# A gated recurrence in halves of 64 tokens: 64x64 scores, and one contraction of 128 rows for the output

## The chip, the cores and the metric

One core of one Trainium2 chip. The time is device microseconds of one execution; what is compared is the median of several executions. A profile is one execution of the same program with the hardware profiler on, and its span is 1 to 2 us shorter than the time on the clock (before: span 646.0, time 647.7). A run is called fast when it lies within 1.5% of the fastest of its kernel. In the profile PE is the matrix engine (TensorE), PEld its weight loads, the granted clock the share of its full clock that PE was given, DVE the vector engine, ACT the scalar engine, POOL GpSimd, and SP the engine whose queue issues most loads.

## The reference, cut to what matters

```python
batch, n_heads, seq, head_dim = (4, 8, 768, 48)
f = 1.0 / (1.0 + np.exp(-f_logit))
for t in range(S):
    state = f[:, :, t, :, None] * state + k_t (outer) v_t      # 48x48 per head
    y[:, :, t] = q_t @ state
x = y, as 3072 tokens x 384
h = x @ w_in                                   # 384 -> 2048
g = h * erf(softplus(h))
out = g @ w_out                                # 2048 -> 384
```

All in 32-bit floats. The recurrence is a small part of the arithmetic, but it feeds everything behind it.

## The kernel before

The 768 tokens of a sequence are cut into 6 chunks of 128; there are 24 chunks, and 3 of them make a block of 384 tokens, the unit of the feed-forward part. Per chunk there are four stages: decays (`stage_d`: a sum over tokens by a matmul with a triangle, then two exponentials), transposes of q' and k' (`stage_t`), scores and state (`stage_s`) and the output y (`stage_y`). With C the sum of the log decays, q' = q exp(C) and k' = k exp(-C), so that masked scores q'k' give the part of y from inside the chunk and q' times the state the rest.

```python
def stage_s(g):
    for a in range(HP):                      # 4 pairs of heads
        for r in range(2):                   # head of the pair
            nc.tensor.matmul(sc[:, r, a, :], lhsT=kT[rows(r), a, :], rhs=qT[rows(r), a, :], ...)   # 48 rows, 128x128
    nc.vector.tensor_tensor(out=A, in0=sc, in1=tri, op=ALU.mult)       # the mask, 128x1024
    if c == NCH - 1:
        return                                # no state after the last chunk
    for a in range(HP):
        for r in range(2):
            nc.tensor.matmul(dS[rows(r), a, :], lhsT=kd[:, h, 0:D], rhs=vt[:, a, r, 0:D], ...)      # 128 rows
    for r in range(2):
        nc.vector.tensor_tensor(out=Sn, in0=dS, in1=old, op=ALU.add)
        nc.gpsimd.tensor_tensor(out=new, in0=Sn, in1=total, op=ALU.mult)  # total: decay over the chunk

def y_matmuls(...):      # out x token, 32 columns of x at a time on four column tiles
    terms.append((pair[:, o : o + M], A[:, r, a, :]))             # v with scores, 128 columns
    if Mbd is not None:
        terms.append((flat[:, M * part : M * (part + 1)], qT[:, a, :]))   # state with q'
```

`total` comes for block 0 from small matmuls, later from rows of exp(C) that eight small DMAs per two chunks carry across partitions (`Tall`).

The feed-forward part is `hidden` (matmuls `hps`, from x) and `project` (matmuls `ops`). The recurrence of block n+1 is laid between the matmuls of block n's hidden and block n-2's project, at fixed slots; the activations and the logits of block n+2 (`prepare`: exp, then ln) are laid there too.

```python
todo = deque(stages(blk))                # the stages of the next block
at = [int(3 + (n - 13) / len(todo) * i) for i in range(len(todo))]   # their slots, n = 96
...
if it + 2 < n_blocks and s == (16 if it < 2 else 30):
    prepare(it + 2, 0, CPB)
```

At the start the weights are loaded and rounded in pieces by DVE, ACT helping; that work, with the early chunks, keeps DVE busy for 116 of the first 139.5 us.

Of the kernel before, what the change touches and what calls it, by code (L numbers as in the profile page):

```python
# [69 lines left out]
def kernel(  # L71
# [19 lines left out]
    M = 32  # L91
    NCH = S // P
# [16 lines left out]
    tri = fixed("tri", [P, P])  # L109
    w_in_sb = fixed("w_in_sb", [P, n_k, d_ff])  # L110
# [58 lines left out]
    epool = main.enter_context(tc.tile_pool(name="epool", bufs=3))  # L169
# [6 lines left out]
    vts = [fixed(f"vt{i}", [P, HP, 2, DP], pool=fix) for i in range(NV)]  # L176
# [5 lines left out]
    Mbds = [fixed(f"Mbd{i}", [P, HP, 2, D], pool=fix) for i in range(2)]  # L182
    Tall = fixed("Tall", [P, n_chunks, HP], pool=fix)
# [16 lines left out]
    def load(g, what="qkv", queue=None):  # L200
        b, c = divmod(g, NCH)
        queue = queue or nc.sync
        for src, t, n in ((q, qns[g % NQ], "q"), (k, kns[g % NQ], "k")):
            if n in what:
                queue.dma_start(out=t[:].rearrange("t (h d) -> t h d", d=D), in_=heads(src, b, c))
        if "v" in what:
            queue.dma_start(
                out=vts[g % NV][:].rearrange("t a r d -> t (a r) d")[:, :, 0:D], in_=heads(v, b, c)
            )

# [80 lines left out]
    xTs, As, qTs, kTs = {}, {}, {}, {}  # L291
# [35 lines left out]
    def stage_d(g):  # L327
        blk, j = divmod(g, CPB)
        if blk == 0:
            both = ps_moe.tile([P, 2, 512], FP32, name="ps_d0", tag="moe")  # L330
            ps, totals[g] = both[:, 0, 0:d_model], both[:, 1, 0:HP]
# [11 lines left out]
        if blk > 0:  # L343
            for a in range(HP):
                nc.sync.dma_start(
                    out=Tall[:, g, a : a + 1],
                    in_=dp[P - 1 : P, 2 * a : 2 * a + 2, :].rearrange("o r d -> o (r d)"),
                )
# [8 lines left out]
    def stage_t(g):  # L357
        pss = []
# [8 lines left out]
        qTs[g] = work.tile([P, HP, P], FP32, name="qT", tag="qT")  # L367
        kTs[g] = work1.tile([P, HP, P], FP32, name="kT", tag="kT")
        nc.scalar.copy(out=qTs[g][:], in_=pss[0][:])  # L369
# [4 lines left out]

    def stage_s(g):
        b, c = divmod(g, NCH)
        qT, kT = qTs[g], kTs.pop(g)
        sc = ps_sc.tile([P, 2, HP, P], FP32, name="sc", tag="sc")
        for a in range(HP):
            for r in range(2):  # L380
                nc.tensor.matmul(  # L381
                    sc[:, r, a, :], lhsT=kT[rows(r), a, :], rhs=qT[rows(r), a, :],
                    start=True, stop=True,
                )
        if g in totals:

            pairs = dps[g % 2][:].rearrange("t (a r) d -> t a (r d)", r=2)
            for a in range(HP):
                nc.tensor.matmul(  # L389
                    totals[g][:, a : a + 1], lhsT=pairs[:, a, :], rhs=ident[:, P - 1 : P],  # L390
                    start=True, stop=True,
                )
            nc.vector.tensor_copy(out=Tall[:, g, :], in_=totals.pop(g))
        A = work1.tile([P, 2, HP, P], FP32, name="A", tag="A")
        nc.vector.tensor_tensor(  # L395
            out=A[:].rearrange("s r a t -> s (r a) t"),
            in0=sc[:].rearrange("s r a t -> s (r a) t"),
            in1=tri[:].unsqueeze(1).broadcast_to((P, H, P)),
            op=ALU.mult,
        )  # L400
        As[g] = A
        if c == NCH - 1:
            return
        dS = ps_at.tile([P, HP, D], FP32, name="dS", tag="at")
        vt, kd = vts[g % NV], kds[g % 2]
        for a in range(HP):
            for r in range(2):
                h = 2 * a + r
                nc.tensor.matmul(  # L409
                    dS[rows(r), a, :], lhsT=kd[:, h, 0:D], rhs=vt[:, a, r, 0:D],  # L410
                    start=True, stop=True,
                )
        new, old = Mbds[g % 2], Mbds[(g + 1) % 2]
        Sn = work1.tile([P, HP, D], FP32, name="Sn", tag="Sn")
        for r in range(2):
            total = Tall[rows(r), g, :].unsqueeze(2).broadcast_to((D, HP, D))
            if c == 0:
                nc.vector.tensor_tensor(
                    out=new[rows(r), :, r, :], in0=dS[rows(r)], in1=total, op=ALU.mult
                )  # L420
                continue
            nc.vector.tensor_tensor(  # L422
                out=Sn[rows(r)], in0=dS[rows(r)], in1=old[rows(r), :, r, :], op=ALU.add
            )
            nc.gpsimd.tensor_tensor(  # L425
                out=new[rows(r), :, r, :], in0=Sn[rows(r)], in1=total, op=ALU.mult
            )

    def stage_y(g):
        c = g % NCH  # L430
# [6 lines left out]
        y_matmuls(y, As.pop(g), vts[g % NV], qTs.pop(g), Mbds[(g + 1) % 2] if c else None)  # L437
        nc.scalar.copy(out=xTs[blk][:, :, j * P : (j + 1) * P], in_=y[:])  # L438

# [3 lines left out]
    def activate(gr):  # L443
# [17 lines left out]
        for _ in range(n):  # L461
# [4 lines left out]
        yield  # L466
# [3 lines left out]
    LEAD = len(SERF_KAB) + 2  # L470
# [89 lines left out]
    def check_decays():  # L560
# [3 lines left out]
            out=low[:], in_=Tall[:].rearrange("p g a -> p (g a)"), axis=AX.X, op=ALU.min  # L564
# [11 lines left out]
    with tc.manual_schedule():  # L576

        use_exp_ln()
# [5 lines left out]
        load_f(2)  # L584
        load_piece(0)
        load(1, "v")
        load(2)
        load_piece(1)
# [7 lines left out]
        )  # L596
        make_identity(nc, ident)
# [4 lines left out]
        for t in vts:  # L602
            nc.vector.memset(t[:, :, :, D:DP], 0.0)
        for t in Mbds:
            nc.vector.memset(t[:], 0.0)
# [56 lines left out]
        stage_y(0)  # L662
        load(3, "v")
# [6 lines left out]
        prepare(1, 0, CPB)  # L670
        load(4, "v")
# [4 lines left out]
        stage_y(2)  # L676
        load(5, "v")
# [271 lines left out]
```

## Time and profile before

| | before |
|---|---|
| time, median (lowest to highest) | 647.45 us (647.44 to 647.85) |
| span of the profile, granted clock | 646.0 us, 0.999 |
| first hidden matmul of block 0 starts at | 32.4 us |
| DVE's last rounding of weights ends at | 139.5 us |

The lines that the prediction rests on stand in it. Three more serve to compare. First the stretch 143 to 197 us, from the table of stretches (length, then busy us of PE, PEld, DVE, ACT, POOL, then granted clock, DMA share, GB/s):

```profile
143.00:197.00 54.00, 53.68 (x321) 33.65 (x322) 41.81 (x35) 46.34 (x40) 7.29 (x6) 1.00 0.17 37
```

PE is idle for 0.3 us in it. Then PE's order of work where hidden of block 0 begins (start, length, engine, line, what, idle time before it):

```profile
32.41 2.85 PE L497 MATMUL hps<-xT,w_in_sb 128*128 128x384 f32 x8 [0.61 <-ACT xT L438]
```

Eight records in 2.85 us. And the loads at the start of the SP queue (start, time the queue spends on issuing, what, how many):

```profile
8.09 0.49 SPq L207 DMA_DIRECT2D vt<-in_v_dram  x1
```

### The profile page before, as it was taken

The page shows a single profiled execution, that of the slowest core. Times are in us where ns is not written, and L with a number is a line of the kernel's source. Part 1 is how long each engine was busy: PE and PEld are TensorE (multiplying, and loading weights), DVE is VectorE, ACT ScalarE, POOL GpSimd, SP SyncE. Part 2 cuts the span into 40 slices and gives each one's busy share as a digit, 9 for nine tenths or more (in the row PEclk, how much of TensorE's full clock was granted, in tenths as well). Part 3 has the DMA queues.
Part 4 walks back from the last instruction along what each step waited for, and adds up shares of the span by engine and source line. Part 5 has one row for each costly group of instructions (what it writes and reads, how often), then busy time and mean ns, then how long its engine had stood idle before and what let it go on. Part 6 is the DMA issues. An engine that isn't in the chain of part 4 may idle for free.

```text
span 646.0 us, 9238 instructions
## 1 busy us (share of the span) xinstructions
PE 630.3 (98%) x3815; PEld 394.4 (61%) x3815; DVE 421.5 (65%) x408; ACT 405.9 (63%) x383; POOL 59.9 (9%) x61
## 2 busy tenths in 40 slices
PE   8999998999999999999999999999999999999996
PEld 7755665656666666666666566666666655555553
DVE  4798998899947765658654677447653686379100
ACT  5446768697888668656775757677564755276100
POOL 0112101111010000202210001100130000000000
PEclk9999999999999999999999999999999999999999
DMA  9995952310114120221202211020000000000101
GB/s 194 248 273 146 271 155 49 66 34 14 25 42 81 26 38 13 62 50 26 38 14 66 44 38 24 13 74 1 2 0 26 13 0 1 37 1 0 38 2 40
DMA packets 120688, 36.89 MB, mean 57 GB/s; under 512 B 112448, under 2 KB 115520, under 8 KB 120640
## 3 DMA queue, kind: packets, MB, share of 16 engines
q1 hardware_dynamic: 118560, 35.84, 24.1%
q10 hardware_dynamic: 2080, 0.39, 0.4%
q8 instruction: 32, 0.52, 0.3%
q14 instruction: 16, 0.13, 0.1%
HBM read 31.46 MB, written 4.72 MB: 56 GB/s over the span
## 4 chain that ended last, share of the span: by engine, by line
PE 89%; DVE 4%; ACT 3%; issue 2%; DMA 1%; SPq 0%; POOL 0%; ACTq 0%; POOLq 0%
PE ops L530 39%; PE hps L497 33%; PE y L145 5%; PE sc L381 3%; PE ps_t L363 3%; PE ps_d L335 2%; PE dS L409 1%; DVE e L159 1%; DVE w_out_sb L274 1%; PE ps_d L325 1%; PE busy L325 1%; DMA Tall<-dp 1%; PE ps_d L389 0%; DVE Hg L283 0%; ACT L299 0%
## 5 line engine op out<-in xcount | busy, mean ns | idle before, releaser
L497 PE MATMUL hps<-xT,w_in_sb 128*128 128x384 f32 x768 | 259.7, 489 | 1.1 <-ACT xT L438 0.6
L530 PE MATMUL ops<-w_out_sb,Hg 128*128 128x384 f32 x768 | 255.9, 489 | 0.0
L530 PEld LDWEIGHTS ops<-w_out_sb,Hg 128*128 128x128 f32 x768 | 143.8, 190 | 97.8 <-issue 2.2
L497 PEld LDWEIGHTS hps<-xT,w_in_sb 128*128 128x128 f32 x768 | 142.7, 190 | 96.0 <-issue 2.2
L159 DVE SCALAR_TENSOR_TENSOR e<-x,e 128x1536 f32<-128x1536 f32 x96 | 173.4, 1806 | 6.0 <-ACT x L154 3.0
L154 ACT ACTIVATE x<-Hg,serf_bias 128x1536 f32<-128x1536 f32 x96 | 147.5, 1569 | 18.8 <-DVE e L159 18.6
L509 DVE COPY Hg<-hps 128x768 f32<-128x768 f32 x48 | 45.9, 956 | 48.9 <-PE hps L497 48.7
L467 DVE TENSOR_TENSOR Hg<-Hg,e 128x1536 f32<-128x1536 f32 x32 | 56.9, 1777 | 11.7 <-ACT e L464 11.6
L353 POOL TENSOR_TENSOR kd<-kn,kd 128x384 f32<-128x384 f32 x21 | 33.0, 1570 | 329.4 <-issue 188.7
L349 DVE TENSOR_TENSOR qd<-qn,dp 128x384 f32<-128x384 f32 x24 | 14.2, 591 | 66.7 <-ACT dp L339 66.7
L151 ACT ACTIVATE e<-Hg,serf_bias 128x1536 f32<-128x1536 f32 x32 | 50.3, 1572 | 0.2
L464 ACT ACTIVATE e<-e 128x1536 f32<-128x1536 f32 x32 | 47.1, 1473 | 0.0
L537 ACT COPY osb<-ops 128x768 f32<-128x768 f32 x8 | 6.4, 796 | 60.4 <-PE ops L530 60.4
L438 ACT COPY xT<-y 128x384 f32<-128x384 f32 x24 | 11.5, 478 | 49.3 <-PE y L145 49.3
L395 DVE TENSOR_TENSOR A<-sc,tri 128x1024 f32<-128x1024 f32 x24 | 29.3, 1221 | 19.0 <-PE sc L381 18.7
L145 PE MATMUL y<-A,vt 128*32 128x128 f32 x768 | 35.2, 277 | 0.1
L339 ACT ACTIVATE dp<-ps_d 128x384 f32<-128x384 f32 x24 | 11.8, 491 | 36.9 <-PE ps_d L335 36.6
L145 PEld LDWEIGHTS y<-A,vt 128*32 128x32 f32 x768 | 27.4, 109 | 12.0 <-issue 6.8
L425 POOL TENSOR_TENSOR Mbd<-Sn,Tall 48x192 f32<-48x192 f32 x32 | 25.8, 807 | 91.0 <-DVE Sn L422 76.3
L369 ACT COPY qT<-ps_t 128x512 f32<-128x512 f32 x24 | 14.0, 582 | 28.7 <-PE ps_t L363 28.6
L381 PEld LDWEIGHTS sc<-qT,kT 48*128 48x128 f32 x384 | 23.3, 187 | 12.5 <-issue 11.3
L145 PE MATMUL y<-qT,Mbd 128*32 128x128 f32 x480 | 30.1, 273 | 0.0
(73 smaller groups left out, 426.2 us busy)
## 6 DMA issues: line engine op xcount, KB each, us to landing
lt<-in_f_logit_dram SPq DMA_DIRECT2D x24, 192.0 KB, 3.9
qn<-in_q_dram SPq DMA_DIRECT2D x24, 192.0 KB, 3.0
Hg<-in_moe_w_out_dram SPq DMA_DIRECT2D x6, 768.0 KB, 5.9
kn<-in_k_dram SPq DMA_DIRECT2D x23, 192.0 KB, 3.3
vt<-in_v_dram SPq DMA_DIRECT2D x23, 192.0 KB, 3.1
w_out_sb<-in_moe_w_in_dram SPq DMA_DIRECT2D x4, 768.0 KB, 6.5
Hg<-in_moe_w_in_dram SPq DMA_DIRECT2D x4, 768.0 KB, 7.8
out_dram<-osb SPq DMA_DIRECT2D x8, 384.0 KB, 2.5
```

The costliest lines, as they stand in the source:

```text
L145: nc.tensor.matmul(y[M * i : M * (i + 1), kt, :], lhsT=terms[n][0], rhs=terms[n][1], start=(n == 0), stop=(n == len(terms) - 1), skip_grou ...
L151: nc.scalar.activation(out=dst[:], in_=h, func=AF.Sigmoid, bias=serf_bias[:, 0:1])
L154: nc.scalar.activation(out=dst[:], in_=h, func=AF.Tanh, bias=serf_bias[:, 1 + i : 2 + i], scale=SERF_KAB[i][0])
L159: nc.vector.scalar_tensor_tensor(out=e[:], in0=x[:], scalar=SERF_KAB[i][2], in1=e[:], op0=ALU.add, op1=ALU.mult)
L353: (nc.vector if blk == 0 else nc.gpsimd).tensor_tensor(out=kd, in0=kns[g % NQ][:].rearrange("t (h d) -> t h d", d=D), in1=kd, op=ALU.mult)
L381: nc.tensor.matmul(sc[:, r, a, :], lhsT=kT[rows(r), a, :], rhs=qT[rows(r), a, :], start=True, stop=True,)
L395: nc.vector.tensor_tensor(out=A[:].rearrange("s r a t -> s (r a) t"), in0=sc[:].rearrange("s r a t -> s (r a) t"), in1=tri[:].unsqueeze(1) ...
L464: nc.scalar.activation(out=e[:], in_=e[:], func=AF.Tanh, scale=SERF_C)
L467: nc.vector.tensor_tensor(out=h, in0=h, in1=e[:], op=ALU.mult)
L497: nc.tensor.matmul(hps[:, j, 0:TB], lhsT=w_in_sb[:, kt, ft * P : (ft + 1) * P], rhs=xTs[blk][:, kt, :], start=(kt == 0), stop=(kt == n_k - 1),
L509: nc.vector.tensor_copy(out=to, in_=hps[:, :, 0:TB])
L530: nc.tensor.matmul(ops[tt // 2][:, tt % 2, 0:d_model], lhsT=gr["h"][:, j, tt * P : (tt + 1) * P], rhs=w_out_sb[:, ft, :], start=(ft == 0), ...
```

## The change

The intent is to take work off PE. A chunk becomes two halves of 64 tokens. Scores between the halves are no longer formed: the state is updated at the middle too, and carries them. Scores are then two 64x64 blocks per head, and y is one contraction over 128 rows, 64 rows of v against masked scores and 64 rows of state against q', where two contractions stood. State increments and scores fill four 64x64 tiles of the array.

```diff
-    ... sc[:, r, a, :], lhsT=kT[rows(r), a, :], rhs=qT[rows(r), a, :]          # 8 of 128x128
+    ... sc[half(c), r, a, :], lhsT=kT[rows(r), a, half(c)], rhs=qA[rows(r), r, a, half(c)]   # 16 of 64x64
-    nc.vector.tensor_tensor(out=A, in0=sc, in1=tri, ...)                        # one mask
+    for c in range(2):
+        for r in range(2):
+            nc.vector.tensor_tensor(out=qA[half(1 - r), r, :, half(c)], in0=sc[half(c), r], in1=tri1[half(c)], ...)
+    next_state(2 * g, dS)                       # state at the middle: 2 DVE adds, 2 POOL products
+    if not last:
+        late[g] = lambda: next_state(2 * g + 1, dS)     # at the end of the chunk: as many again
...
+    nc.tensor.matmul(y[M * i : M * (i + 1), kt, half(c)],
+                     lhsT=sv[:, r, c, a, o : o + M],     # v of 64 tokens over the 48 rows of state
+                     rhs=qA[:, r, a, half(c)], ...)      # masked scores over q'
...
+def load_sv(g, queue=None):      # v once more, beside the state's rows: four loads per chunk
+    for r in range(2):
+        for c in range(2):
+            (queue or nc.sync).dma_start(out=svs[g % NS][half(1 - r), r, c, :, PAD : PAD + D],
+                                         in_=v[b, r::2, t0 : t0 + C, :]...)
...
-    epool = ... name="epool", bufs=3          # the activations' accumulators
+    epool = ... name="epool", bufs=2          # room for sv; activations spread to suit
-        for _ in range(n):      LEAD = len(SERF_KAB) + 2      step = s % 4 == 2
+        for _ in range(n + 1):  LEAD = len(SERF_KAB) + 3      step = s % 7 in (2, 5)
...
+    ADJACENT = 3        # from block 3 on, y of a chunk and scores of the next stand side by side
+            if blk == ADJACENT:
+                todo = [(stage_s, g0)]
+                elif blk < ADJACENT: todo += [(stage_d, g + 1), (stage_s, g), (stage_t, g + 1), (stage_y, g)]
+                else:                todo += [(stage_d, g + 1), (stage_t, g + 1), (stage_y_s, g)]
```

Cut: the decay rows `Tall` for the middle too (sixteen small DMAs where there were eight), q' copied by ACT in two halves, the triangle without its corner, buffers renamed. v is still loaded as before as well, for the state increments.

## The prediction

> **What bounds the kernel now.** I read the page from the top, then a table of stretches, then the chain of waits inside one steady block, then the queue of loads at the start.
>
> ```profile
> PE 630.3 (98%) x3815; PEld 394.4 (61%) x3815; DVE 421.5 (65%) x408; ACT 405.9 (63%) x383; POOL 59.9 (9%) x61
> PE 89%; DVE 4%; ACT 3%; issue 2%; DMA 1%; SPq 0%; POOL 0%; ACTq 0%; POOLq 0%
> ```
>
> TensorE is busy almost throughout and carries 89% of the chain that ended last. But a mean hides stages, so the stretches come next (columns: PE, weight load, DVE, ACT, POOL, clock, DMA share, GB/s):
>
> ```profile
> 0.00:38.00 38.00, 33.07 (x374) 26.85 (x374) 25.36 (x54) 18.51 (x31) 5.41 (x13) 1.00 1.00 221
> 38.00:75.00 37.00, 35.24 (x345) 23.15 (x342) 33.59 (x43) 25.18 (x34) 7.28 (x8) 1.00 0.85 225
> ...
> 96.00:143.00 47.00, 44.37 (x328) 27.66 (x326) 40.81 (x48) 38.21 (x41) 7.25 (x7) 1.00 0.26 48
> ...
> 265.00:342.00 77.00, 77.00 (x471) 47.87 (x472) 46.47 (x42) 52.48 (x47) 11.04 (x9) 1.00 0.19 40
> ```
>
> Two regimes. From about 143 us on, PE has no idle time and the others are at 60 to 70%: a microsecond less on PE is a microsecond less in all. Before 143 us, where the weights are rounded, DVE is at 87 to 91% and the DMA engines are full until 38 us: there less PE work need not pay.
>
> What a chunk of 128 tokens costs on PE, from the chain of waits in a steady block (start, us, what):
>
> ```profile
> 289.84 0.65 PE ps_d L335 x2
> ...
> 294.36 1.09 PE sc L381 x16
> 295.45 0.49 PE dS L409 x16
> 295.94 4.71 PE hps L497 x14
> 300.66 0.87 PE ps_t L363 x8
> 301.53 4.52 PE hps L497 x14
> 306.05 1.69 PE y L145 x56
> ...
> 383.05 1.03 PE y L145 x32
> ```
>
> Scores, state increment and y are 1.09 + 0.49 + 1.69 = 3.27 us per chunk; y has 56 records, 32 in the first chunk of a sequence, which has no state. The same 14 hps records take 4.52 us in plain mode and 4.71 us just after tiled ones: leaving tiled work costs about 0.2 us. Rates: 14 records of 384 columns in 4.52 us is 0.323 us, 0.84 ns per column, so 107 ns for 128 columns; y at 1.69/56 = 30 ns per record therefore runs close to four records at once, scores at 68 ns close to two.
>
> **What the Trainium skill says.** "TensorE: Matmul & The Clock Gate", Part 3 (packing small matmuls): matmuls on different tiles of the array run concurrently, a few ns apart. This trace agrees for four column tiles (y) and for two row tiles (scores); no run so far shows row and column tiles together in one 64x64 arrangement, which the change needs. The same page, section "Wait — 56ns, not 53.3ns?": start to start never falls below about 25 ns for small matmuls. Here dS has 16 records in 0.49 us, 31 ns with its drain, so the trace neither binds nor clears that floor for what the change wants, 12 to 15 ns. "TensorEngine Tiling (Array Packing)", Key Properties: changing the tiling mode drains the engine; the 4.71 against 4.52 us above agrees. "GPSIMD Engine Reference", Specifications: its SBUF interface is shared with VectorE; the state multiply on POOL takes 498 to 1909 ns for one shape here, which fits.
>
> **The change part by part, on PE.**
> y: the state and the scores share the 128 rows, so one matmul does what two did, but each moves 64 columns. Per half: 12 output slices of 32, 4 of them over two heads, 16 matmuls; 32 per chunk, 64 records (two per fp32 matmul, as 56 for 28 now). At 64 x 0.84 + 2 = 56 ns and four at once: 64/4 x 56 = 0.90 us. The same model gives 56/4 x 109 = 1.53 for the present y, measured 1.69, so 0.16 of entry and drain is added: 1.06. Saved: 0.63 us; nothing in a first chunk (32/4 x 109 = 0.87 against 0.90).
> sc: 32 records of 64 columns instead of 16 of 128. The weight load sets the pace here: 8 decay sums that move one column each take 1.05 us in the timeline, the last of them 0.25, so (1.05 - 0.25)/7 = 0.11 us per load of 128 columns, and 64 columns take about 58 ns. On four tiles 32/4 x 58 = 0.46 against 0.89. Saved: 0.43.
> dS: 32 records of 48 columns on four tiles instead of 16 on two: both about 0.36. Last chunks of a sequence, which had none, get 16 records: +0.36. One change of mode between sc and dS goes: -0.15.
> Sum for an ordinary chunk: 0.63 + 0.43 + 0.15 = 1.21. From block 3 on, y and the next scores stand side by side, one excursion from plain mode less: about 0.2 saved. 1.42 us.
> Chunks 9 to 23 are in the steady part: 10 ordinary x 1.42 = 14.2; two first ones x 0.79 = 1.6; three last ones x 0.9 = 2.7. Sum 18.5 us. ps_d and ps_t do not change, nor do hps and ops, 80% of PE.
>
> **Added elsewhere.** DVE: four masks of 64x256 instead of one 128x1024 (1.22 us). Taking 0.15 us fixed and 1.04 ns per element from the state add (192 elements, 350 ns), 4 x 0.42 = 1.67, +0.45. Two state updates instead of one: two more adds, +0.70. So +1.15 us of DVE per chunk, and two more POOL multiplies of 0.5 to 1.9 us. ACT: the q' copy in two halves, each 512 elements, +0.58. In the steady part that is 17 us over 360 on DVE: hidden. In the six chunks of blocks 1 and 2 it is 7 us on an engine with under 11 idle us between 38 and 143; PE's saving there, 6 x 1.2, is therefore not credited. The activations are spread (six steps between groups instead of five, 26 steps per block instead of 22): by counting slots the last group of block 0 is ready two slots (1.3 us) before it is needed; with DVE lagging 1 to 4 us there, one wait of about 2 us.
> DMA: v is loaded a second time (four loads per chunk) and eight decay rows instead of four are moved. 196,608 bytes at 221 GB/s are 0.9 us. Five such loads stand before the first decay rows in the queue, which is full then:
>
> ```profile
> 40.94 6.01 SPq L196 DMA_DIRECT2D lt<-in_f_logit_dram  x3
> 47.06 6.06 SPq L345 DMA_DIRECT2D Tall<-dp  x8
> ...
> 52.64 1.60 POOL L425 TENSOR_TENSOR Mbd<-Sn,Tall 48x192 f32<-48x192 f32 x2 [9.04 <-DMA Tall<-dp]
> ```
>
> Now this wait is harmless: the state made at 52.64 is first read by the next chunk's y, at 62.41. After the change y of chunk 3, which ran at 48.99, reads the state of its own middle. The rows would be issued at 47.1 + 4.5 = 51.6, the multiply could start about 5.5 us later (52.64 - 47.06) at 57, and y at 59: a wait of about 9 us on PE, of which I take 5 to 6 as lost, since DVE, the other bound there, catches up meanwhile. Against it: ps_t no longer waits for the state add to free its PSUM buffer (4.9 us in the list of waits), as dS moves to the scores' banks.
>
> **Sum.** Steady -18.5, block-0 activation +2, early part +5: about -11.5, 636 us.
>
> **Rivals.**
> (a) Clean gain: the early waits are filled by what DVE and PE lag anyway, and the PE saving counts there too. For: PE idles only some 5 us between 38 and 143 us. Then -20 to -25: 623 to 628.
> (b) Issue-bound PE: if records cannot start faster than 25 ns, y takes 1.6 us and sc and dS 0.8 each; the steady gain is gone or reversed. For: the skill's floor. Against: y's bursts of 4 within one 109 ns period. Then 645 to 655.
> (c) The start becomes the bound: 5 extra loads, doubled decay rows and a serial chain masks, add, multiply, y in the dense blocks 0 to 2 cost 12 us or more. For: DVE at 91%, DMA at 1.00. Then 640 to 645.
>
> **Range and chances.** My sum is the middle; (a) gets a quarter, (b) and (c) together about as much. The line for 2% is 634.5, just under my value: 636 us, range 625 to 647. Chances: faster 0.43, same 0.52, slower 0.05.
>
> **What would show it.** y 64 records in 1.0 to 1.1 us and sc with dS about 0.9 to 1.0 us in a steady block; if they are near 1.6 each, (b). PE busy about 19 us less after 143 us. A wait of PE on y of chunk 3 near 50 to 60 us behind POOL and the decay rows; if y runs there at once, (a). DVE busy up by about 28 us. Blocks 1 and 2 ending near 148 instead of 143 us. I am wrong if PE idles in the steady part behind DVE's four masks, or if the early part moves by more than 10 us either way.

## The result, and the profile after

| | before | after |
|---|---|---|
| median of 4 runs, same chip | 647.65 us (647.44 to 648.26) | 663.88 us (663.30 to 664.79) |
| ratio after/before | | 1.025 (95%: 1.0232 to 1.0268) |

A ratio here is the mean time of one kernel's fast runs over the mean of the other's of the same rounds, so it is not quite the ratio of the medians. The kernel became slower by 2.5%, 28 us from the predicted 636 us, and outside the range of 625 to 647.

The page of the changed kernel, its busy times, its clock and the chain that ended last:

```profile
PE 618.4 (93%) x4871; PEld 384.3 (58%) x4871; DVE 454.3 (69%) x525; ACT 416.7 (63%) x405; POOL 92.1 (14%) x120
...
PEclk9759999899799999999999999999999999999999
...
PE 72%; DVE 15%; issue 5%; DMA 3%; ACT 2%; SPq 1%; POOL 1%; DVEq 0%; ACTq 0%; POOLq 0%
```

PE has 12 us less work (630.3 before), yet it is busy for 93% of the span, not 98%. On the chain that sets the end it fell from 89% to 72%, and DVE rose from 4% to 15%: PE now waits. And the clock row, all nines before, has two 7s, a 5 and an 8 in the first half: the granted clock falls there.

The stretches, same windows as before:

```profile
0.00:38.00 38.00, 26.96 (x436) 23.60 (x436) 24.18 (x56) 16.95 (x28) 7.57 (x21) 0.84 0.88 194
38.00:75.00 37.00, 28.86 (x330) 17.80 (x330) 25.65 (x38) 15.81 (x24) 8.84 (x10) 0.84 0.76 188
...
143.00:197.00 54.00, 46.25 (x322) 27.30 (x321) 41.35 (x50) 36.96 (x34) 9.82 (x10) 0.91 0.22 41
...
265.00:342.00 77.00, 77.00 (x620) 47.72 (x619) 54.51 (x60) 54.51 (x51) 11.51 (x16) 1.00 0.29 55
```

The last line is the regime the prediction worked out: PE full, clock 1.00. The first three are where PE idles (11.0, 8.1 and 7.8 us, against 4.9, 1.8 and 0.3 before), at a clock of 0.84 to 0.91.

The starts of each block's first hidden matmul in the two traces place the difference. A stretch runs from one block's first hidden matmul to the next's:

| from | before, us | after, us | difference |
|---|---|---|---|
| start to hidden of block 0 | 32.4 | 45.5 | +13.1 |
| 1st stretch | 50.6 | 55.5 | +4.9 |
| 2nd stretch | 49.5 | 49.6 | +0.1 |
| 3rd stretch (recurrence of block 3) | 77.8 | 93.2 | +15.4 |
| 4th to 7th (blocks 4 to 7) | 76.8, 77.0, 76.8, 75.5 | 73.1, 73.2, 73.2, 70.6 | -16.0 |
| the rest | 129.6 | 129.2 | -0.4 |
| span | 646.0 | 663.1 | +17.1 |

So the gain is there, 16.0 us in twelve chunks, and twice as much is lost before it. In steady work the chain of waits shows the new matmuls (start, us, what):

```profile
302.56 1.03 PE y L489 x64
303.59 0.51 PE sc L434 x32
304.09 0.48 PE sc L442 x32
```

y with 64 records takes 1.03 us where 56 took 1.69; the state increments (line 434; they share the tile `sc`) take 0.51 and the scores 0.48. Together 2.02 us for 3.27 before.

What PE waited for, from the list of waits (total us, times, longest):

```profile
PE hps L556 <- DVE Hg L568: 7.1, 2, 6.3
PE y L489 <- DMA sv<-in_v_dram: 6.6, 1, 6.6
PE y L489 <- ACT qA L395: 5.4, 2, 3.4
...
PE ops L589 <- DVE Hg L526: 3.4, 1, 3.4
```

The first is in the main one wait (6.3 of 7.1 us), the second and the last are one each. The second stands at the start: the v rows of chunk 2 come late. PE's order there:

```profile
42.43 2.48 PE L489 MATMUL y<-qA,sv 128*32 128x64 f32 x64 [6.64 <-DMA sv<-in_v_dram]
45.48 5.00 PE L556 MATMUL hps<-xT,w_in_sb 128*128 128x384 f32 x8 [0.57 <-ACT xT L493]
```

After the wait the same 64 records take 2.48 us, not 1.03, and the eight hidden records 5.00 us, not 2.85: PE runs at half rate, single records 0.64 us apart where they stand 0.32 us apart elsewhere. The Trainium skill, "TensorE: Matmul & The Clock Gate", Part 1, has the array's clock halved after a window of about 3.4 us in which it is idle. The rate agrees here; but the half rate began before the long wait. In this trace the granted clock is either 1.00 or 0.50. Before the change it is 1.00 as long as PE works; here it is 0.50 in six stretches of 3.4 to 20.5 us, 44.3 us together, with PE busy for 31.0 of them. Two of the six:

```profile
29.40:49.90 20.50, 11.98 (x149) 9.13 (x150) 11.77 (x21) 3.60 (x4) 4.06 (x6) 0.50 0.97 222
...
162.50:172.70 10.20, 6.04 (x10) 3.32 (x11) 7.16 (x6) 8.97 (x8) 4.11 (x2) 0.50 0.03 0
```

The first begins at 29.4 us, after idle pieces of 0.95, 0.23 and 0.95 us, and the wait of 6.64 us begins at 35.8. If work at half clock takes twice as long, about 15 of the 31.0 us are its price on PE (an estimate; part of it may lie where PE would have waited anyway): 22.1 of the 31.0 us lie before hidden of block 2, 8.9 in the third stretch. Waits thus cost more than their own length.

The queue of loads that the wait points to:

```profile
7.11 2.78 SPq L227 DMA_DIRECT2D sv<-in_v_dram  x4
...
15.55 4.01 SPq L227 DMA_DIRECT2D sv<-in_v_dram  x4
...
36.99 2.65 SPq L227 DMA_DIRECT2D sv<-in_v_dram  x4
...
57.62 11.25 SPq L368 DMA_DIRECT2D Tall<-dp  x16
```

The four loads of one chunk hold the queue for 2.65 to 4.01 us, though they carry only 48 KB each. Up to 60 us a single one takes 0.59 to 0.80 us, except one of 2.03 at 15.55; why that one is longer is not shown. Those of chunk 2 are reached at 37.0 us. The queue before the change reaches the same place at 30.4; the two sets ahead of it, 2.78 and 4.01 us, make up the difference.

The third stretch has three waits, from PE's order of work:

```profile
166.66 8.42 PE L556 MATMUL hps<-xT,w_in_sb 128*128 128x384 f32 x16 [6.35 <-DVE Hg L568]
...
198.27 0.66 PE L388 MATMUL ps_t<-ident,kd 128*128 128x128 f32 x4 [1.87 <-POOL kd L376]
...
214.24 2.93 PE L589 MATMUL ops<-w_out_sb,Hg 128*128 128x384 f32 x4 [3.44 <-DVE Hg L526]
```

The first is at a buffer of PSUM, the memory that PE writes to, that DVE empties late (the copy `Hg<-hps`); 16 hidden records then take 8.42 us, where 14 took 4.52 before. The second is at k', made late; the third at the activation's last product. In the whole stretch PE is idle for 13.2 us (0.5 before) and does 8.9 us of its work at half clock (none before). The experiments below take the second and the third wait away and shorten the first.

### The profile page after: what moved, and what is told of

Its sections match the earlier page's. It is cut to its first block, busy times and chain, and to the rows that moved or that the text cites. A ratio compares the mean times of both kernels' runs of the same rounds, so it can differ in the third digit from the quotient of the medians.

```text
span 663.1 us, 11920 instructions
## 1 busy us (share of the span) xinstructions
PE 618.4 (93%) x4871; PEld 384.3 (58%) x4871; DVE 454.3 (69%) x525; ACT 416.7 (63%) x405; POOL 92.1 (14%) x120
## 4 chain that ended last, share of the span: by engine, by line
PE 72%; DVE 15%; issue 5%; DMA 3%; ACT 2%; SPq 1%; POOL 1%; DVEq 0%; ACTq 0%; POOLq 0%
PE ops L589 35%; PE hps L556 27%; DVE e L164 3%; PE y L489 3%; PE ps_t L388 2%; DVE qA L460 2%; PE ps_d L356 1%; DMA lt<-in_f_logit_dram 1%; PE sc L442 1%; PE sc L434 1%; DVE Hg L304 1%; DVE w_out_sb L295 1%; DVE sv L415 1%; DMA sv<-in_v_dram 1%; DVE w_out_sb L309 1%
## 5 line engine op out<-in xcount | busy, mean ns | idle before, releaser
L556 PE MATMUL hps<-xT,w_in_sb 128*128 128x384 f32 x768 | 266.6, 500 | 7.7 <-DVE Hg L568 7.1
L556 PEld LDWEIGHTS hps<-xT,w_in_sb 128*128 128x128 f32 x768 | 146.4, 195 | 106.9 <-DVE Hg L568 8.3
L164 DVE SCALAR_TENSOR_TENSOR e<-x,e 128x1536 f32<-128x1536 f32 x96 | 172.8, 1800 | 17.3 <-ACT x L159 15.4
L159 ACT ACTIVATE x<-Hg,serf_bias 128x1536 f32<-128x1536 f32 x96 | 146.0, 1566 | 0.3
L416 POOL TENSOR_TENSOR sv<-sv,Tall 48x192 f32<-48x192 f32 x80 | 54.1, 676 | 250.7 <-DVE sv L415 101.9
L460 DVE TENSOR_TENSOR qA<-sc,tri 64x256 f32<-64x256 f32 x96 | 40.5, 422 | 30.2 <-PE sc L442 28.5
L372 DVE TENSOR_TENSOR qd<-qn,dp 128x384 f32<-128x384 f32 x24 | 15.8, 659 | 42.9 <-ACT dp L360 42.9
L489 PE MATMUL y<-qA,sv 128*32 128x64 f32 x1536 | 30.9, 232 | 14.2 <-DMA sv<-in_v_dram 6.6
L489 PEld LDWEIGHTS y<-qA,sv 128*32 128x32 f32 x1536 | 25.9, 117 | 27.3 <-issue 14.3
L360 ACT ACTIVATE dp<-ps_d 128x384 f32<-128x384 f32 x24 | 11.8, 491 | 36.5 <-PE ps_d L356 34.1
L395 ACT COPY qA<-ps_t 64x512 f32<-64x512 f32 x48 | 27.7, 576 | 10.2 <-PE ps_t L388 9.7
L493 ACT COPY xT<-y 128x384 f32<-128x384 f32 x24 | 11.5, 479 | 33.5 <-PE y L489 33.3
L415 DVE TENSOR_TENSOR sv<-sc,sv 48x192 f32<-48x192 f32 x80 | 28.4, 354 | 2.2
L156 ACT ACT_TABLE_LOAD x17 | 21.8, 1283 | 6.5 <-DVE Hg L526 6.2
```

What stands on the lines that cost most here:

```text
L156: nc.scalar.activation(out=dst[:], in_=h, func=AF.Sigmoid, bias=serf_bias[:, 0:1])
L159: nc.scalar.activation(out=dst[:], in_=h, func=AF.Tanh, bias=serf_bias[:, 1 + i : 2 + i], scale=SERF_KAB[i][0])
L164: nc.vector.scalar_tensor_tensor(out=e[:], in0=x[:], scalar=SERF_KAB[i][2], in1=e[:], op0=ALU.add, op1=ALU.mult)
L415: nc.vector.tensor_tensor(out=new, in0=add, in1=old, op=ALU.add)
L416: nc.gpsimd.tensor_tensor(out=new, in0=new, in1=total, op=ALU.mult)
L460: nc.vector.tensor_tensor(out=qA[half(1 - r), r, :, half(c)], in0=sc[half(c), r], in1=tri1[half(c)].unsqueeze(1).broadcast_to((C, HP, C)), ...
```

## The experiments

Three theories stood against each other for the loss: (A) the activations' part of the change (two accumulators, other pacing) makes the third stretch late; (B) the loads of v and the extra work of DVE and POOL make the start late, and the lateness of the rounding runs on into the third stretch; (C) the side-by-side order costs by itself in the block where it begins. Besides the total, each run gives the same stretches; all runs differ from the changed kernel ("after") unless said otherwise. The recorded expectations letter their theories anew: there C is the loads of v, D the longer serial chain, E and G variants of B. Where the start code is the same as after's, or differs in the place of one stage (e4, e11), the first hidden matmul began at 42.9 to 45.5 us (five traces), so a shift of under 3 us at the start says nothing. (The 46.5 and 36.9 us in some expectations were misread: the traces have 45.5 for after and 37.6 for e2.)

| run | first hidden | 1st | 2nd | 3rd | 4th | 5th | total, us |
|---|---|---|---|---|---|---|---|
| before | 32.4 | 50.6 | 49.5 | 77.8 | 76.8 | 77.0 | 647.65 |
| after | 45.5 | 55.5 | 49.6 | 93.2 | 73.1 | 73.2 | 663.88 |
| e1, before with after's activations | 32.9 | 50.6 | 47.5 | 81.9 | 76.8 | 77.0 | 652.55 |
| e2, no v loads | 37.6 | 55.1 | 49.5 | 94.8 | 73.1 | 73.2 | 657.63 |
| e3, v rows copied by POOL | 40.4 | 56.3 | 50.1 | 94.9 | 74.6 | 73.2 | 663.43 |
| e4, three accumulators | 44.0 | 55.8 | 49.7 | 89.7 | 73.1 | 73.1 | 660.07 |
| e5, first 9 chunks as before | 32.2 | 50.6 | 49.4 | 86.6 | 73.1 | 73.1 | 638.91 |
| e6, e5 with two accumulators | 33.0 | 50.6 | 47.5 | 90.8 | 73.1 | 73.2 | 642.64 |
| e7, never side by side | 44.1 | 55.9 | 49.9 | 84.9 | 73.7 | 73.7 | 659.27 |
| e8, no second state update early | 42.8 | 51.7 | 50.9 | 92.5 | 73.1 | 73.2 | 659.03 |
| e9, change from chunk 12 | 32.2 | 50.6 | 49.4 | 77.8 | 77.4 | 73.1 | 636.65 |
| e10, change from chunk 9 | 33.0 | 50.6 | 49.4 | 76.4 | 77.4 | 73.1 | 634.31 |
| e11, e4, side by side from block 4 | 43.9 | 56.2 | 49.8 | 81.1 | 78.8 | 73.1 | 657.50 |
| e12, filler matmuls | 42.5 | 55.1 | 50.9 | 92.9 | 73.1 | 73.2 | 662.53 |
| e13, logits' tables moved | 42.9 | 54.9 | 51.2 | 89.9 | 73.1 | 73.2 | 659.92 |
| e14, e10 with the same move | 32.5 | 50.6 | 49.4 | 76.4 | 74.3 | 73.1 | 630.49 |
| e15, v loads of a quarter | 42.7 | 55.9 | 49.8 | 93.5 | 73.1 | 73.2 | 662.99 |
| e16, chunk 2's v by ACT's queue | 39.5 | 59.3 | 50.0 | 93.9 | 73.1 | 73.2 | 663.33 |

The stretches come from the traces. e9, e10 and e14 were timed in three rounds; every other experiment is a single look, beside one to seven runs of the kernel before.

### e1: the activations' part alone, on the kernel before

```diff
-    epool = ... name="epool", bufs=3
+    epool = ... name="epool", bufs=2
-        for _ in range(n):
+        for _ in range(n + 1):
-    LEAD = len(SERF_KAB) + 2
+    LEAD = len(SERF_KAB) + 3
-                    step = s % 4 == 2
+                    step = s % 7 in (2, 5)
```

> The kernel before with the activation part of the change alone: two e buffers instead of three, one step more before the last tanh, six steps between groups, 26 steps per block. Theory A (the two e buffers cost the 15 us that the third stretch, the first with the second product, grew by: 78 to 93 us): this kernel is slower than before by 8 us or more, about 656 to 662, with ACT waiting tens of us for the product that frees e. Theory B (DVE is overloaded by the added masks and adds, the buffers are harmless): within 3 us of before, 645 to 650.

Measured: 652.55 us, +5.0; the 2nd stretch 2.0 shorter, the third 4.1 and the 6th, not in the table, 2.1 longer. That lies between the two expectations: theory A holds for a part of the 15.4 us, not for most of it.

### e2: no second loads of v

```diff
     def load_sv(g, queue=None):
+        return
```

> The changed kernel without the second load of v (the v rows of the joint operand stay zero: a wrong result on purpose). Theory C (the four small loads per chunk clog the queue at the start: they took 2.7 to 4.0 us of its issue time each time, not the 0.9 us of their bytes): the first hps matmul comes at 36 us or earlier instead of 46.5, and the whole gains 9 to 14 us, about 650 to 655. Rival D (the longer serial chain scores, four masks, adds, POOL products, y sets the start): first hps at 43 or later and a gain under 4 us.

Measured (wrong: v is missing from the output): 657.63 us, 6.2 less. Start and gain lie between the two expectations. The first hidden matmul starts at 37.6, at least 4.9 us earlier than in any trace with these loads in the SP queue, and the wait on `sv` is gone. DVE is the check on theory B: until its last rounding it is busy for 129.1 us and idle for 30.1 after, busy 129.4 and idle 21.7 here, busy 116.1 and idle 23.3 before. The loads cost DVE 8 us of waiting; the 13 us of further work in that time is not theirs. Of the 15.4 us in the third stretch nothing came back (94.8), so the loads make the start late but not the third stretch.

### e3: the same rows copied by POOL from the first load of v

```diff
-                (queue or nc.sync).dma_start(out=svs[...], in_=v[...])
+                nc.gpsimd.tensor_copy(out=svs[...], in_=vts[g % NV][half(c)] ...)
```

> The changed kernel with the v rows copied on chip by POOL from the v that is already loaded (four copies of 64x192 per chunk) instead of loaded again; the result stays right. Theory C: first hps near 36 to 38 us, whole 650 to 656, unless POOL's copies slow DVE[...], then DVE busy grows by more than 10 us. Rival D: first hps at 43 or later, no gain.

Measured: correct, 663.43 us: no gain. The start is earlier (40.4), and the 1st, 3rd and 4th stretches give it back. PE's wait on the `sv` loads is gone, but at the same y it now waits 2.69 us for POOL's state; that POOL's copies delay it is argued, not shown. As a mend this was a miss.

### e4: three accumulators again

```diff
-    epool = ... name="epool", bufs=2
+    epool = ... name="epool", bufs=3         # room made by narrower sv and shared q, k buffers
-        for _ in range(n + 1):  LEAD = len(SERF_KAB) + 3   step = s % 7 in (2, 5)
+        for _ in range(n):      LEAD = len(SERF_KAB) + 2   step = s % 4 == 2
```

> The changed kernel with the activations as before: three e buffers, five steps between groups, 22 steps per block. The room comes from padding the joint operand on one side only (64 instead of 80 columns) and from keeping q and k of chunks 2 and 5 in the output buffer. Theory A: the third stretch falls from 93 to below 83 us, the whole to 650 to 654. Theory B: the third stretch stays above 88 us and the whole at 660 or more.

Measured: correct, 660.07 us; the third stretch 3.5 us shorter, and its wait of 3.44 us at `ops` is gone. With two accumulators, that last wait is theirs. But the stretch stays at 89.7, as theory B had it: the accumulators are the smaller part.

### e5 and e6: the first nine chunks in the old form, with three and with two accumulators

```diff
+    G0 = 9
     def stage_s(g):
+        if g < G0:
+            return old_s(g)        # the kernel before's stage_s; stage_y likewise
```

> The first nine chunks (blocks 0 to 2, where weights are rounded) in the form of before, whole chunks with separate score and state products, and the changed form from chunk 9 on, with three e buffers and the pacing of before. Theory E (the loss is all made before the third stretch ends, by work added to DVE and to the load queue while DVE rounds weights; the steady part gains about 3.7 us per block as measured): the first hps at 32 to 33 us, the third stretch 74 to 78 us, whole 628 to 634, better than both. Rival F (the changed form costs something in the third stretch also without the rounding load, as its chunks begin there): the third stretch above 82 us, whole above 638.

> The same with the activations of the change (two e buffers, six steps). If the buffers cost what they cost on the kernel before (5 us in run e1): 3 to 6 us more than e5, 632 to 639. If the two only collide with the overloaded DVE: within 1 us of e5.

Measured: 638.91 and 642.64 us. Both results are wrong, relative error 0.24: the old form with the new triangle, which lacks its corner. No instruction changes in number or shape by that, so the times are used; e10 has it right. The start is at 32 to 33 us again, as before the change, so all of the late start comes from the changed form in the first nine chunks. But the third stretch is 86.6 and 90.8 us, not 77.8, though nothing early is late: theory B does not reach there alone.

### e7: never side by side

```diff
-    ADJACENT = 3
+    ADJACENT = 99
```

> The changed kernel with y and the next scores never side by side (the order of blocks 1 and 2 in all blocks). By my sum adjacency is worth 0.2 us per chunk: 15 chunks, steady stretches 73.8 instead of 73.2 us, whole +2 to +4 us. Rival: side by side the two send DVE a burst and cost stalls in the third stretch: then that stretch shortens by 3 us or more and the whole is faster.

Measured: correct, 659.27 us; the third stretch 84.9, so 8.3 us less, and each steady stretch 0.6 longer (the last of them 1.6). Theory C holds: standing side by side is worth 0.2 us a chunk later, as predicted, and costs 8 us once where it begins.

### e8: no second state update in the first nine chunks

```diff
-        if not last:
+        if not last and g >= 9:
             late[g] = lambda: next_state(2 * g + 1, dS)
```

> The changed kernel without the second state update in chunks 0 to 8 (a wrong result on purpose): eight times two adds of 0.35 us less on DVE, 5.7 us, and as many POOL products less. Theory E: DVE sets the pace until the last weight is rounded, so the last rounding ends 4 us or more earlier than 160.3 us and the whole is 4 to 8 us faster. Rival (loads and ACT set it): under 2 us.

Measured (wrong): 659.03 us. DVE's work until its last rounding falls by 7.3 us (129.1 to 121.8) and the rounding ends 5.8 us earlier; start and 1st stretch together are 6.5 us shorter, of which the 2.7 at the start lie within its spread. The third stretch keeps 92.5, and the whole gains 4.9. So the second state updates cost some 4 to 5 us early on; the run takes their POOL products away too and does not part them from the adds.

### e9 and e10: the change from chunk 12 or chunk 9 on only

```diff
+    G0 = 9                                     # 12 in e9
+    trib = fixed("trib", [P, P])               # triangle without corner, for chunks from G0 on
+    if g < G0: return old_s(g)                 # and old_y
-    ADJACENT = 3
+    ADJACENT = 4
-    bufs=2 (accumulators), other pacing
+    bufs=3, pacing as before
     # v rows loaded into sv from chunk G0 on; buffers of the old form share sv's room
```

> The form of before (with its full triangle for the running sums, which e5 lacked) for chunks 0 to 11, the changed form from chunk 12 on, side by side with the next scores there; three e buffers, pacing of before. Theory G (the changed form pays wherever DVE and the load queue have slack, and the loss up to the third stretch is from placing it where they have none): start and first three stretches as before (32, 50.6, 49.5, 78 us), then 73.1 per stretch and 70.6: about 632 to 635, correct. Rival: the switch of forms or the changed order costs a stall in the fourth stretch, above 76 us, and the whole stays above 638.

> As e9, but the changed form from chunk 9 on, with y and the next scores apart in that block. If adjacency alone made the third stretch of e5 long (86.6 us; e7 gained 8 us there by taking it away), it is 75 to 78 us here and the whole 629 to 633. If the masks and adds right behind the rounding matter too, 79 to 84 us and no better than e9.

Measured: both correct, both somewhat slower than expected, by their fourth stretch; 636.65 us (ratio 0.9837, 95% 0.9813 to 0.9861) and 634.31 us (0.9803, 0.9771 to 0.9835). The third stretch is 77.8 and 76.4. Four single traces now take it apart, one cause at a time: 76.4 (e10), 86.6 with side by side begun a block earlier (e5), 90.8 with two accumulators as well (e6), 93.2 with the changed form in the early chunks as well (after). The changed form in the early chunks is worth 2.4 us there by this order, 3.1 between e5 and e4, and 4.7 between e10 and e11: far less than theory B had it. In e10 the side-by-side order begins one block later, and the fourth stretch then is 77.4 us where the following ones are 73.1: a part of the cost of beginning moves along with it.

### e11: after, three accumulators, side by side from block 4

```diff
-    bufs=2 (accumulators), ADJACENT = 3
+    bufs=3, pacing as before, ADJACENT = 4
```

> The changed form everywhere, with three e buffers and the pacing of before, side by side only from block 4 on. e4 gained 3.8 us and e7 8.3 us in the third stretch: if they add, that stretch is 80 to 83 us and the whole 650 to 654; the start stays at 46 us.

Measured: correct, 657.50 us, against 650 to 654 expected; third stretch 81.1 as expected, fourth 78.8 (73.1 after). A part of the stall moves into the block where the order begins, as in e10.

### e12: PE kept busy ahead of y of chunk 2

```diff
-            keep_busy(3)
+            keep_busy(16 if g == 2 else 3)
```

> The changed kernel with 16 filler matmuls instead of 3 ahead of y of chunk 2, where PE waits some 7 us and then runs eight hps records at half the rate (0.64 us apart instead of 0.32). If the granted clock is what a wait costs twice, those records come 0.32 us apart and the first stretch shortens by 2 to 3 us, 661 to 662. If not, no change.

Measured: 662.53 us, a gain of 1.4. The filler ended 2.6 us before the v rows came, and of the eight hidden records after it a part still ran at half rate (4.35 us for eight; 5.00 after, 2.85 before). Half rate on these eight records is worth at most 2.2 us (5.00 against 2.85). Over the whole run PE still did 29 us of work at half clock (31.0 after), so this run is no test of what half clock costs in all; no run is.

### e13 and e14: the logits' exp and ln moved beside the decay's exponentials

The trace of ACT in the block where the order begins shows table loads (`ACT_TABLE_LOAD`; L360 and L363 are the decay's exponentials, L337 and L338 exp and ln of the logits, L159 a tanh):

```profile
184.21 1.28 ACT L320 ACT_TABLE_LOAD   x1
186.60 1.16 ACT L337 ACTIVATE lt<-lt 128x1152 f32<-128x1152 f32 x1 [1.10 <-DVE lt L333]
187.79 1.16 ACT L338 ACTIVATE lt<-lt 128x1152 f32<-128x1152 f32 x1
188.96 1.28 ACT L159 ACT_TABLE_LOAD   x1
190.26 3.04 ACT L159 ACTIVATE x<-Hg,serf_bias 128x1536 f32<-128x1536 f32 x2
193.31 1.28 ACT L320 ACT_TABLE_LOAD   x1
194.61 0.49 ACT L360 ACTIVATE dp<-ps_d 128x384 f32<-128x384 f32 x1
```

The same table is loaded at 184.21 for the logits and again at 193.31 for the decay, with a tanh between. In the blocks after it, and in the kernel before, both stand at slot 30 and share one load: with 12 stages, the before kernel puts the decay of the second chunk at 3 + 83/12 x 4 = 30, and with 9 stages it is 3 + 83/9 x 3 = 30. With the ten of the first side-by-side block it is 3 + 83/10 x 4 = 36. The Trainium skill, "ScalarE: Activation LUTs", section "Table sets: the hidden batching unit", says to do all of one set before switching; here a list longer by one entry broke that.

```diff
-                if it + 2 < n_blocks and s == (16 if it < 2 else 30):
+                if it + 2 < n_blocks and s == (16 if it < 2 else 36 if blk == ADJACENT else 30):
```

> The changed kernel with one edit: in the first block whose chunks lie side by side, the logits' exp and ln of the next block are moved beside the decay exponentials (slot 36 instead of 30), so that they share one table load as they do in every other block. Theory (separate table loads make the decay late and TensorE waits at the transposed k): the third stretch falls from 93.2 to about 89 us and the total by 3 to 5 us, with no wait of over 1 us on the decay there. Rival (the vector engine's list of work in that block is what is late, the tables only lie beside it): under 1 us of change.

> The change from chunk 9 on with chunks side by side from block 4 (634.3 us), and the same move of exp and ln in that first block. Theory: its fourth stretch of hidden falls from 77.4 to about 73.9 us and the total to about 631 us. Rival: 634 us unchanged within 1 us.

Measured: e13 correct, 659.92 us, third stretch 89.9 (93.2), and the waits at the transposes are gone. PE's order there in e13, to be set beside the line at 198.27 shown above:

```profile
191.60 0.60 PE L388 MATMUL ps_t<-ident,qd 128*128 128x128 f32 x4
192.04 0.60 PE L388 MATMUL ps_t<-ident,kd 128*128 128x128 f32 x4
```

e14 is correct, 630.49 us (630.32 to 630.62), ratio 0.9738, 95% 0.9722 to 0.9754. Its fourth stretch fell from 77.4 to 74.3. The table theory holds at 3.1 to 3.3 us in both kernels. This version beats both kernels, by 17 us and by 33 us. Its page:

```profile
PE 612.4 (97%) x4463; PEld 382.3 (61%) x4463; DVE 442.3 (70%) x484; ACT 414.4 (66%) x397; POOL 90.2 (14%) x103
```

PE's work is 17.9 us under the kernel before's, where the prediction had 18.5 for these chunks (9 to 23), and is again nearly all of the span. The clock is 1.00 throughout PE's work, and the third stretch has 2.1 us of PE idle.

### e15: as many v loads, a quarter of the bytes

```diff
-                    out=svs[g % NS][half(1 - r), r, c, :, PAD : PAD + D],
-                    in_=v[b, r::2, t0 : t0 + C, :]...
+                    out=svs[g % NS][half(1 - r), r, c, 0:1, PAD : PAD + D],
+                    in_=v[b, r : r + 1, t0 : t0 + C, :]...
```

> The changed kernel with the same number of v loads, each of a quarter of the bytes (the result is wrong on purpose). If the number of loads is what makes the start late, the first hidden product still starts at 45 to 46.5 us; if it is the bytes or the descriptors of each load, it starts at 38 to 41 us, as it did at 36.9 us without any loads, and the total falls by 4 to 6 us.

Measured (wrong): 662.99 us; first hidden at 42.7, which is 0.2 us before the earliest of the traces with the same start, so no effect is shown. The SP queue with 12 KB loads:

```profile
7.03 2.71 SPq L227 DMA_DIRECT2D sv<-in_v_dram  x4
...
15.19 3.98 SPq L227 DMA_DIRECT2D sv<-in_v_dram  x4
```

2.71 and 3.98 us, against 2.78 and 4.01 with four times the bytes: a load's time in the queue does not come from its bytes. Their number is what is left, and there are twenty of them before the first decay rows; no run varied the number alone, but without them (e2) those rows are issued at 46.6 us, with them at 57.6.

### e16: chunk 2's v loads issued by ACT

```diff
-        load_sv(2)
+        load_sv(2, nc.scalar)
```

> The changed kernel with one edit: the four v loads of chunk 2 are issued by the scalar engine instead of standing in the sync engine's queue behind the loads of weights; their number and bytes stay. If their place in that queue makes y of chunk 2 wait (6.6 us at 42.4 us), the first hidden product starts at 37 to 40 us instead of 44 to 46.5, and the total falls by 4 to 6 us. Rival (the transfers themselves are slow while the DMA engines are full): it starts at 43 us or later.

Measured: correct, first hidden at 39.5 us, 3.0 us before the earliest (e12) and 6.0 us before the latest trace with those loads in the SP queue, and the wait on `sv` is gone: their place in that queue was the cause. But the total is 663.33 us; the 1st stretch grew to 59.3. There, in PE's order of work, stands a wait that after did not have:

```profile
39.48 5.49 PE L556 MATMUL hps<-xT,w_in_sb 128*128 128x384 f32 x8 [0.58 <-ACT xT L493]
...
63.20 0.43 PE L489 MATMUL y<-qA,sv 128*32 128x64 f32 x4 [3.89 <-POOL sv L416]
```

And POOL, which makes that state, waited for the decay rows:

```profile
62.65 1.08 POOL L416 TENSOR_TENSOR sv<-sv,Tall 48x192 f32<-48x192 f32 x2 [8.51 <-DMA Tall<-dp]
```

This is the wait at y of chunk 3 that the prediction named. In after it is hidden by an earlier one: the state is made at 62.93 us there, 62.65 here, and PE comes to that y at 63.76 anyway. Take the first wait away and the second appears. e16 also shows eight hidden records in 5.49 us, at a clock of 0.50 from 38.8 us on, after idle pieces of 1.23 and 0.88 us with short bursts between: one gap of 3.4 us was not needed here.

## Why the prediction was wrong, by its own steps

The sum was -11.5 us; the spans differ by +17.1. Of the 28.6 us between, 11.1 lie in the start and the first two stretches (+7 predicted with the +2 of the activations, +18.1 measured) and 19.2 in the third stretch (-3.8 predicted, the share of chunks 9 to 11 in the 18.5; +15.4 measured). The rest went 1.7 us better than predicted.

**Chunks 9 to 11 counted as steady: the step that cost most.** "From about 143 us on, PE has no idle time", "a microsecond less on PE is a microsecond less in all", and DVE's added work "hidden", hold from block 4 on. In the third stretch PE was idle for 13.2 us, behind DVE's copy, late k' and late activation products, and did 8.9 us of work at half clock. With the old order of stages and three accumulators (e10) the same chunks in the new form take 76.4 us, 2.1 of them idle.

**PE's saving from block 4 on: right.** y was to take 1.06 us and took 1.03; state increments and scores were to take 0.9 to 1.0 us together and took 0.99 to 1.03. The 1.42 us per ordinary chunk gives 14.7 us for chunks 12 to 23 by the prediction's sum (eight ordinary at 1.42, two first at 0.79, two last at 0.9); the 4th to 7th stretches gave 16.0. Rival (b), issue-bound PE, fell: 64 records in 1.03 us are 16 ns each. DVE's work grew by 33 us (421.5 to 454.3), predicted 28, and in steady work it was hidden, as said.

**The loads: the step that failed first in time.** "196,608 bytes at 221 GB/s are 0.9 us" priced a chunk's four loads by bytes. They take the queue 2.65 to 4.01 us (e15: whatever their bytes). The prediction's own profile held the measure: "47.06 6.06 SPq L345" was eight loads of half a kilobyte each, so 0.76 us a load at next to no bytes. Counted so, five chunks' loads are 20 x 0.7 = 14 us of queue, not 4.5. The first decay rows, predicted at 51.6 us, were issued at 57.6.

**The early part, +5: wrong in size and in place.** It measured +18.1 us (start 13.1, 1st stretch 4.9, 2nd 0.1). The prediction sought the wait at y of chunk 3 and took the start up to 32 us as unmoved; the wait came at y of chunk 2, 6.64 us, because its v rows stood at 37 us in the queue, and half clock from 29.4 us on; the clock is in no term of the prediction. e2 shows at least 4.9 us of the start for the loads, e16 that their place in the queue makes the wait; e8 gives 3.8 us in the 1st stretch, up to 6.5 with the start, for the second state updates. These overlap and are not to be added, and what share each has of the 18.1 is not settled. The predicted wait was real, and masked (e16).

**DVE before 143 us: seen, and charged too little.** The prediction's 87 to 91% for DVE hold from 38 us on (25.36 of the first 38 us are 67%). It called DVE "an engine with under 11 idle us" there, took PE's saving out, and charged nothing more. The last rounding ended 19.8 us later (139.5 to 159.3): 13.0 us of added work and 6.8 us more of waiting. "Blocks 1 and 2 ending near 148 instead of 143" was the same error: hidden of block 2 began at 150.6 instead of 132.5.

**Activations, +2: the right term, too small.** The wait that it named is there, 2.20 us at `ops` in e1 (3.44 after). But by itself this part costs 5.0 us (e1), where 3.4 us of work at half clock follow that wait; in the third stretch 3.5 to 4.2 us are the accumulators (e4, e6).

**Side by side, -0.2 a chunk: right, with a cost left out.** It saves 0.2 a chunk (e7: 0.6 per stretch of three), and costs 8.3 to 10.2 us where it begins in block 3 (e7; e5 against e10), 4.3 to 5.7 where it begins in block 4 (the fourth stretches of e10 and e11 against 73.1). The prediction read the list of stages for what it saves and did not place the extra entry in the slots. 3.1 to 3.3 us of this are the second table load (e13, e14). A second part is the first wait of the third stretch, PE at `hps` behind DVE's copy: 6.35 us after, 5.97 with three accumulators (e4), 4.34 without side by side (e7), 2.80 with it but nothing late (e5), 1.29 with neither (e10). So side by side is worth 1.5 to 2.0 us of it, and the lateness of DVE about 3. The extra `stage_s` puts 2.5 us of masks and adds just ahead of that copy; that this burst is the cause is argued from the order in the trace, as no run moved the burst alone. A third part is the clock: in the third stretch e5 does 8.4 us of work at half clock, about 4 us lost by the estimate above, and e10 none; e7 does 8.0, hardly less than after's 8.9. In e5 these pieces follow the waits at the copy and at the transposes; no run parts the clock from the waits.

**Rivals and range.** Rival (c), the start becomes the bound, was the right one for the early part, where its "12 us or more" takes in the 18.1 measured. It was worked out to 640 to 645 because the loss in the third stretch was not seen, and got too small a chance.

## What to carry to other kernels

A change that takes work off the bound engine is to be laid where that engine is the bound: the same change from chunk 9 on, with its buffers and table loads kept as they were, gives 630.49 us, and from chunk 0 on 663.88. Count small loads by their number in the queue and ask for each what stands before it, and when a schedule's list grows by one entry, work out the new slot of every other entry: what shared a table or a buffer may no longer do so. A wait that is not there may only be hidden by an earlier one, so the next profile is read for new waits, not only for the one taken away. And when PE starts to idle, look at its granted clock: here 31.0 us of its work ran at half of it.

## What the Trainium skill lacked or had wrong

- "TensorE: Matmul & The Clock Gate", section "Wait — 56ns, not 53.3ns?", has start to start never below about 25 ns for small matmuls. On four column tiles 64 records of 64 columns took 1.03 us, 16 ns each, and on four 64x64 tiles 32 records took 0.48 to 0.52 us, 15 to 16 ns each, drain included. For matmuls on different tiles the floor doesn't bind, as Part 3 of the same page would have it.
- The same page, Part 1 (and its advice on idle gaps of over about 3 us): the half rate agrees (0.64 for 0.32 us per record), but in e16 it came after gaps of 1.23 and 0.88 us among short bursts. A longest harmless gap alone does not predict it; the page names frequent short idle pieces as a second way to it, without a figure.
- "DMA: Bandwidth & Descriptors", section "Issuing engines are not separate DMA queues", calls the time to initiate a DMA usually small beside the DMA. For one load that agrees: one of 48 KB held its queue for 0.6 to 0.8 us (once 2.0), of a median of 4.2 us from issue to landing. But in one queue these times add up: the twenty loads held it for 14.8 us, about the same per load at 12 KB, while at the 221 GB/s of this start 48 KB are 0.22 us. That page has no measured figure on this chip for the time one small load occupies its queue; the one it gives stands in its section on trn3, for earlier chips as a group.
- "ScalarE: Activation LUTs", section "What ACT_TABLE_LOAD costs": the 1283 ns per load agree (1.28 us). The further drain of about 1380 ns per switch does not show: a load at 188.96 follows work that ended at 188.95, and the next activation starts at 190.26, so the switch took 1.31 us.
